# New tables of order for the two recurrences of an attention-with-memory training step

## The chip, the cores and the metric

The kernel runs on one core of a Trainium2 chip. The metric is the device time of one execution in microseconds. Three runs of the kernel before took 2881.65, 2874.34 and 2867.66 us, so the median is 2874.34 us. A separate execution was taken by the hardware profiler; all rows of the trace are from it.

The engines are named as the profile names them: PE multiplies matrices, PEld loads its weights, DVE, ACT and POOL work on vectors, and SP issues transfers between DRAM and the on-chip memory. Each engine runs its own instructions in the order in which the program lists them, and waits on semaphores for the others.

## The reference

The reference is one forward pass and its gradients. A layer norm of `x` (2048 tokens of 512) feeds two branches that are added to `x`: a dense layer with a squared relu, and an attention that runs over segments of 32 tokens and carries 8 memory rows from one segment to the next.

```python
for s in range(n_seg):                       # 64 segments of 32 tokens, 32 heads of 128
    h = concatenate([mem, xs])               # 8 memory rows and 32 tokens
    q, k, v = h @ Wq, h @ Wk, h @ Wv
    p = softmax(where(mask, q @ k.T * scale, -1e9))
    o = (p @ v) @ Wo
    mem, out = o[:8], o[8:]
...
return x + A(layernorm(x)) + B(layernorm(x))
```

The output and the gradients to ten inputs are returned. Since `mem` of one segment comes from the segment before, the forward pass is a chain of 64 steps, and its gradient is a chain of 64 steps in the other direction.

## The kernel before

The program has four parts: the dense branch, the forward recurrence, the backward recurrence, and a last part with the weight gradients and the layer norm's gradient. The change touches only the two recurrences.

**Steps and blocks.** Four segments make a block, so each recurrence has 16 blocks of four steps. The step of one segment is written by `chain` (L1510 for the forward pass, L1895 for the backward pass), and ends with small matmuls (L1574 and L1967) whose result a copy on DVE (L1578 and L1970) puts into the input of the next step. Beside the chain there is work of a block that no step waits for at once: `l_qkv` and `l_attn` for the 32 memory rows of the block, `dw_unit` with weight gradients of the dense branch, and in the backward pass `l_pre` and `l_post`. PE runs this work between the pieces of the chain.

**Where the plan's order comes from.** Every piece of work is given to `_Plan.add` (L427) with the engines on which it may run and the keys that it reads and writes. `_Beat.run` (L571) then sets the order. A table gives each piece of a block one number. The number divided by four is its place, in units of 10 ps, and the remainder chooses the engine where several are possible. A block is shifted by `_FWD_BEAT` or `_BWD_BEAT`. The pieces are taken from a heap by place, each as soon as all pieces that it depends on have been taken (L575 to L591), and written into the engines' streams in that order. So the numbers set an order and choose engines. They are no waits, and no time of them reaches the chip. Each recurrence has three tables: one for the blocks in the middle, one for the first block and one for the last.

**The pieces that the prediction follows.** In the backward pass `l_post` (L1801) works for a block that is already behind the chain. It calls `post` twice, with t=1 and t=2. Each call has four rows of loads (`load_x`, L1825): `xs` (256 KB from `S_Q` or `S_GON`) and `ys` (64 KB from `S_DSL` or `S_PL`). Two groups of 16 matmuls (L1852) each need two rows. Both calls use the same tiles, so the loads of t=2 can only start when the matmuls of t=1 are done. `load` (L1881) brings in `qN` (`XA<-S_Q`) and `kN` (`XA<-S_K`) for the next step, and `part_bd` (L1919) stores gradients (`S_GN<-XK`) for the last part. All these transfers are issued by SP, in one order.

In the forward pass `l_attn` stores `oLN` (`S_ONL<-XN`, L1500) from a tile into which the next block's `l_qkv` writes its first result; the copy that writes it must wait until the store has read the tile.

Of the kernel before, what the change touches and what calls it, by code (L numbers as in the profile page):

```python
# [29 lines left out]
        -35108400, -35109600, -34069200, -33215600, -34203599, -27704800, -27740400, -27741600, -27857600, -28116799,  # L30
        -22391600, -32365600, -34834799, -26164400, -34263999, -30979200, -31039600, -28224400, -28490000, -35299599,
        -24862400, -25241200, -24694800, -24696000, -23745199, -23655600, -27293600, -28702399, -24296000, -23041599,
        -24794400, -24795600, -24804400, -24862400, -23065199, -21676800, -20583200, -21155600, -19949600, -20989199,
        -18652400, -34074800, -37341200, -22558400, -21219600, -30884798, -22557600, -21218400, -22739998, -20980400,
        -28366398, -21035600, -21178799, -20605600, -19862000, -23279200, -19503199, -20900398, -20943198, -20102799,
        -20601998, -20944398, -25291598, -17164398, -22294798, -19283199, -24175997, -19087199, -24174797, -24467597,
        -19211598, -21183197, -21320797, -20775600, -24605198, -21543200, -21144400, -23337598, -21143200, -21144400,
        -21177599, -20788400, -22347998, -20771600, -20561999, -31007600, -19832400, -26897200, -17555199, -21206798,
        -20530798, -19731599, -21187198, -19222398, -18641598, -17183598, -19206798, -21250398, -22817199, -21321997,
        -17842399, -23020797, -23019597, -24468797, -23904799, -18536000, -16712398, -18133597, -28483597, -24721598,  # L40
        -16714798, -23417200, -18662000, -16232000, -17364000, -16018398, -17676799, -16228000, -18608398, -15828000,
        -18532798, -20371200, -17828800, -53166400, -22479600, -25422400, -11184000, -22650800, -14834800, -9430800,
        -27846000, -29697200, -14539200, -20660400, -27866000, -18134400, -19296800, -26897600, -17455600, -25411200,
        -32264400, -22280800, -18564000, -33130400, -16210800, -17698000, -25142800, -16899600, -14704800, -16240000,
        -12004800, -12012000, -20302000, -12007200, -12006000, -25868800, -11752400, -13070800, -20175200, -6536400,
        -8713200, -10025600, -6537600, -6171600, -12362800, -6540000, -5040000, -13676800, -6250800, -1146800,
        -15441200, -5170000, -1148000, -10122000, -3590000, 56800, -10009600, -3342400, 55600, -6087600, -2657200,
        573200, -4985199, -5052797, 1297201, 9000803, -1145600, -31999, -1979997, 2555600, 3227201, 2138803,
        -46612000, -41546397, -38099999, -29635598, -23431599, -22088399, -15200000, -15202400, -22613198, -15052400,
        -15051200, -29632799, -14813200, -14008398, -14838400, -17825599, -22861600, -13897200, -13094000, -22466799,  # L50
        -13347198, -13588798, -13111199, -12667198, -13144398, -12759598, -11490398, -12012398, -13987197, -15031197,
        -12011198, -13082799, -20575997, -17271999, -16903597, -16901999, -12015600, -11391998, -15051200, -15048800,
        -21121599, -15028400, -15029600, -17823199, -14466800, -17299999, -14423200, -13642798, -14468000, -12118000,
        -12119200, -21241599, -13139598, -13348398, -13092399, -12110398, -12112798, -12111598, -11683598, -11286398,
        -16066797, -15186397, -11947598, -15185197, -16157599, -22449599, -12741199, -15767197, -12007200, -11630398,
        -10745597, -22755997, -11401998, -16980398, -11753600, -12008400, -10721200, -11753600, -11232798, -10564799,
        -10301600, -9523198, -10300800, -9425598, -9757600, -16181600, -22719600, -14226400, -15694800, -18456000,
        -9370000, -10520000, 16840800, -13515198, -10210400, -10183600, -17245199, -10208800, -10302000, -17641998,
        -9415200, -9435999, -9414000, -16200398, -8681600, -8678800, -8154400, -10645999, -9479998, -9480798,
        -8328799, -10191598, -12689598, -10190398, -6047598, -6952798, -12719197, -9317598, -7609599, -10184397,  # L60
        -10191598, -6362799, -11621597, -8842397, -6360800, -6173198, -9859600, -10303200, -11002398, -9416000,
        -9417200, -9479999, -9268000, -17542799, -8806800, -11970398, -8676400, -7768000, -8155600, -6411999,
        -9482398, -10190398, -7783199, -9601598, -9600398, -9553198, -9507598, -9602798, -6302799, -19317597,
        -6374797, -9230797, -6221199, -9508798, -6829197, -5222799, -5076000, -6063198, -5104397, -23340397, -6070798,
        -5085598, -4551600, -4772000, -4626400, -4627600, -6497599, -6217998, -4131200, -6139198, -3946000, -3821598,
        -12406000, -8649600, -16295200, -15608800, -8648800, -5695200, -13044400, -4524800, 28582800, -3549600,
        -3553200, -5107598, -3551200, -3594800, -10185198, -3334800, -4316798, -3341200, -5105999, -2522000, -2397200,
        -1882400, -7007599, -5040398, -6653598, -6261999, -1571998, -1571998, -1570798, -1267998, 8802, -10331199,
        -8691197, -6289597, -1266798, -6259999, -5227199, -5084799, -6258797, -1506400, 446802, -3418000, -3419200,
        -5104799, -3536000, -3552400, -20737998, -2898400, -6402798, -3057600, -5086399, -1905600, -1355200, -1356400,  # L70
        -7977599, -5182398, -1764398, -3248399, -1441998, -1472398, -1492798, -37198, -361998, -6281997, -451598,
        -5972397, -7821597, -4999197, -5224399, -5990797, -3337199, -2988400, 452802, -6249597, -8347997, 435202,
        451602, 55600, 182800, 181600, -25200, 795602, 1229601, -3509600, 2090402, 1128800, 2176402, 2145600,
        -2782400, -18027600, -8857200, -1200, -5668800, 636000, 161600, 3070400, 471200, 7186802, 13911600, 23484800,
        -55200, 13365600, -17325600, -18465600, 3230800, 3899600, 122000, -6523600, 7050802, 8038402, 6965601,
        9318402, 3474802, -358398, 11142000, 8637602, 11321600, 11236800, 11319200, 11318000, 12418401, 12383601,
        5885600, 11175602, 10658402, 12636400, 2772400, 13057600, 13941600, 15736800, 16727600, 16725200, 16724000,
        17085201, 8694800, 13290800, 20578800, 22906403, 26035203, 9340800, 29804803, 24149203, 30399200, -40125200,
        -45562397, -13558400, -12482400, 10973602, 9985602, 5080000, -1928000, -8948000, -3944000, 7572003, 2804003,
        3576003, 1208003, -640000, -2712000, 2896000, 4788002, 460002, -531999, 9428002, -4391998, 7656002, 7748000,  # L80
        4748002, 19136000, 18468000, 18468000, 3896000, -3776000, 4360002, 13844002, 21888000, 21888000, 27368000,
        30636000, 28140000, 27296000, 22820000, 24276000, -291999, 37320003, 8000003, 8400003, -664000, 308001,
        -644000, -515998, -36000, -6283999, 64000, 464002, -1348000, -4723999, 64000, -9399998, 2328000, 3092002,
        2308000, 2656002, -7688000, 5680001, 2348000, -10039999, 132000, 8092001, 4892000, 6532002, 5368000, 3692001,
        -5344000, 9368002, 12660000, 18344002, 11404000, 8092001, 24936000, -5551999, -5595999, 5920000, -6795999,
        -991998, 5400000, -5587998, 4360002, 7476000, -5587998, -7139998, 8272000, 1712001, -5751998, 11356000,
        -16859998, -12599999, 12932000, -11211999, 6536002, 14852000, -11703999, -631998, 13096000, -6843998, 6504002,
        12468000, -395998, -1107999, 15328000, -6787998, -631998, 15904000, 5624001, -9979998, 15872000, -1723999,
        1332002, 14652000, -175999, 5220002, 18368000, -1903999, 2168001, 22100000, 940001, 2232002,
    ),  # L90
# [2109 lines left out]
```

## Time and profile before

| | us |
|---|---|
| median of 3 runs | 2874.34 |
| lowest and highest run | 2867.66, 2881.65 |
| the profiled execution, its own time | 2858.24 |
| span of the profiled execution, first to last instruction | 2856.5 |

The profiled execution was some 16 us shorter than the median run. Its span is 1.7 us shorter than its own time. A row of the trace's timeline has the start in us, the length in us, the engine, the line, the operation with what it writes and reads, and a count; in brackets stands how long the engine sat idle before it and what ended that. A row of the waits has who waited for whom, the total in us, how often, and the longest.

### The profile page before, as it was taken

To read this page: it belongs to the slowest core of one execution; us is meant where nothing else is said; L and a number is where in the kernel's file an instruction comes from. 1 tells how busy PE (TensorE), PEld (TensorE's weight loads), DVE (VectorE), ACT (ScalarE), POOL (GpSimd) and SP (SyncE) were. 2 spreads that over 40 slices of the span, in tenths; PEclk is the share of its full clock that TensorE was granted. 3 is DMA by queue.
4 is the path that set the end of the run, shared out by engine and by line. 5 is a ranking of instruction groups with operands and counts; after the bars stand their busy time and mean duration, and the time that the engine had idled before them with its cause. 6 is when DMAs were issued, how large, how long until landed. Compare 5 with 4: busy or idle time off the path is not lost.

```text
span 2856.5 us, 114006 instructions
## 1 busy us (share of the span) xinstructions
PE 2690.7 (94%) x47470; PEld 1553.5 (54%) x47640; DVE 1632.8 (57%) x4814; ACT 1168.5 (41%) x2761; POOL 929.7 (33%) x2595
## 2 busy tenths in 40 slices
PE   7998999999999999899899999999999999999999
PEld 5664565655656555655555555555555544444444
DVE  5644666666666666776666666666666602232322
ACT  4333454555555555554455455455555400000000
POOL 1112223223322223344444445444444301111111
PEclk9999999999999999999999999999999999999999
DMA  6657768777777764568888888998898899788861
GB/s 195 211 170 206 198 196 216 207 204 200 202 206 207 204 182 162 157 159 213 221 237 224 221 236 227 212 230 221 226 226 219 225 350 291 228 255 267 253 185 44
DMA packets 558171, 606.25 MB, mean 212 GB/s; under 512 B 229925, under 2 KB 359222, under 8 KB 555606
## 3 DMA queue, kind: packets, MB, share of 16 engines
q1 hardware_dynamic: 542486, 544.88, 69.5%
q0 software_dynamic: 15168, 54.08, 6.0%
q8 instruction: 373, 6.11, 0.9%
q14 instruction: 144, 1.18, 0.1%
HBM read 290.14 MB, written 272.12 MB: 197 GB/s over the span
## 4 chain that ended last, share of the span: by engine, by line
PE 28%; issue 10%; DVE 8%; DMA 5%; POOL 2%; ACT 2%; SPq 0%; DVEq 0%; POOLq 0%; ACTq 0%
PE ps L2137 12%; PE ps L1752 7%; PE ps L871 3%; PE ps L981 3%; DMA S_GN<-XK 1%; DMA WA<-S_GN 1%; DVE maskA L1938 1%; PE ps L757 1%; DVE XN L854 1%; DMA XN<-S_PL 1%; PE ps L1967 1%; DVE XA L1936 1%; DVE XN L761 1%; DVE PB L1943 1%; DVE PB L1942 1%
## 5 line engine op out<-in xcount | busy, mean ns | idle before, releaser
L871 PE MATMUL ps<-WA,PA 128*32 128x512 bf16 x6144 | 367.2, 380 | 4.7 <-DVE PA L1578 3.8
L2137 PE MATMUL ps<-WA,WB 128*128 128x512 bf16 x1505 | 330.7, 379 | 2.2 <-DVE gwo L761 0.6
L1752 PE MATMUL ps<-WA,XK 128*32 128x512 bf16 x5120 | 319.3, 383 | 5.5 <-DVE XK L854 3.4
L871 PEld LDWEIGHTS <-PA 128*32 128x32 bf16 x8192 | 206.9, 96 | 202.3 <-issue 15.7
L2137 PEld LDWEIGHTS <-WB 128*128 128x128 bf16 x1896 | 185.6, 98 | 224.6 <-issue 1.1
L997 POOL COPY BDA<-PB 32x128 bf16<-32x128 bf16 x484 | 139.9, 289 | 422.1 <-DVE PLp L1546 288.5
L761 DVE CAST gwo<-ps 128x512 bf16<-128x512 f32 x64 | 40.0, 684 | 401.7 <-PE ps L2137 268.3
L763 ACT CAST gwo<-ps 128x512 bf16<-128x512 f32 x64 | 33.2, 598 | 517.1 <-PE ps L2137 357.8
L763 ACT CAST XK<-ps 128x512 bf16<-128x512 f32 x313 | 180.4, 587 | 102.5 <-PE ps L981 42.1
L1752 PEld LDWEIGHTS <-XK 128*32 128x32 bf16 x5120 | 117.9, 97 | 145.6 <-DVE XK L854 44.8
L1752 PE MATMUL ps<-WA,XN 128*32 128x512 bf16 x2560 | 168.2, 382 | 0.5 <-issue 0.2
L2148 POOL DMA_DIRECT2D out_dram<-gwo x96 | 71.4, 751 | 295.4 <-ACT gwo L763 264.4
L761 DVE COPY XN<-ps 128x256 f32<-128x256 f32 (+1 forms) x148 | 66.5, 450 | 169.7 <-PE ps L757 118.5
L763 ACT CAST XA<-ps 128x512 bf16<-128x512 f32 (+1 forms) x154 | 90.3, 587 | 127.9 <-PE ps L871 114.9
L763 ACT COPY XN<-ps 128x512 bf16<-128x512 bf16 (+1 forms) x156 | 72.6, 477 | 158.1 <-PE ps L1752 54.4
L871 PE MATMUL ps<-WB,PA 128*32 128x512 bf16 x2048 | 127.5, 386 | 9.8 <-issue 9.0
L1417 PE MATMUL ps<-WB,OT 128*32 128x256 bf16 x4096 | 131.8, 274 | 4.8 <-DVE OT L854 3.8
L981 PEld LDWEIGHTS <-XK 128*128 128x128 bf16 x1536 | 95.1, 98 | 69.1 <-issue 21.2
L1630 PE MATMUL ps<-XA 128*128 128x512 bf16 x353 | 115.5, 381 | 10.3 <-issue 4.6
L1417 PEld LDWEIGHTS <-OT 128*32 128x32 bf16 x4096 | 101.4, 97 | 40.1 <-DVE OT L854 28.5
L854 DVE STREAM_TRANSPOSE XK<-XK 128x256 f32<-128x256 f32 x256 | 108.5, 434 | 24.8 <-ACT XK L763 21.9
L1003 POOL COPY BDA<-XA 32x256 bf16<-32x256 bf16 x256 | 107.2, 419 | 46.2 <-POOL XK L1003 13.9
(302 smaller groups left out, 5571.8 us busy)
## 6 DMA issues: line engine op xcount, KB each, us to landing
S_GN<-XK SPq DMA_DIRECT2D x192, 256.0 KB
WA<-S_GN SPq DMA_DIRECT2D x160, 256.0 KB
S_K<-kN SPq DMA_DIRECT2D x64, 256.0 KB
S_Q<-qN SPq DMA_DIRECT2D x64, 256.0 KB
S_V<-vN SPq DMA_DIRECT2D x64, 256.0 KB
S_ON<-oN SPq DMA_DIRECT2D x64, 256.0 KB
XA<-S_K SPq DMA_DIRECT2D x64, 256.0 KB
XA<-S_Q SPq DMA_DIRECT2D x64, 256.0 KB
```

Source lines behind the costliest of these rows:

```text
L761: nc.vector.tensor_copy(out, in_)
L763: nc.scalar.copy(out, in_)
L854: self.plan.add({"DVE": 0.36}, lambda e, x=x: nc.vector.transpose(dst[:, x, :, :].rearrange("p i c r -> p (i c r)").bitcast(F32).rearrange ...
L871: nc.tensor.matmul(bk()[32 * j:32 * (j + 1), :], lhsT=win(dc), rhs=Wt(dc, c0), start=(dc == 0), stop=(dc == DC - 1), tile_position=(0, 32 ...
L981: nc.tensor.matmul(bv()[:, n * P:(n + 1) * P], lhsT=B_[:, i, :, :].rearrange("p j k -> p (j k)"), rhs=X[:, i, :], start=(y == 0 and n == 0 ...
L997: self.plan.add({"ACT": 0.31, "DVE": 0.2, "POOL": 0.31}, lambda e, j=j: {"ACT": nc.scalar.copy, "DVE": nc.vector.tensor_copy, "POOL": nc.g ...
L1003: self.plan.add(cost or {"ACT": 0.4, "DVE": 0.27, "POOL": 0.42}, lambda e, j=j: {"ACT": nc.scalar.copy, "DVE": nc.vector.tensor_copy, "POO ...
L1417: nc.tensor.matmul(bk()[32 * t:32 * (t + 1), :], lhsT=tq(OTt, i, j), rhs=Wo[:, JQ * i + j, h * HB:(h + 1) * HB], start=(i == 0 and j < 2), ...
L1630: A(pe(0.217, "f", 0.11), lambda e, c=c, z=z, x=x: nc.tensor.matmul(bks[x]()[:], lhsT=anT[x][:, c, :], rhs=sx[z][:], start=(c == 0), stop= ...
L1752: nc.tensor.matmul(bk()[32 * j:32 * (j + 1), :], lhsT=tq(XT, i, j), rhs=wtf(t, i, j), start=(first and i == 0), stop=(last and i == NI - 1 ...
L2137: nc.tensor.matmul(bks[n]()[:], lhsT=HNc[:, rc, dc * P:(dc + 1) * P], rhs=half_of(gns[y], hf), start=(y == 0), stop=(y == NRC - 1))
L2148: q.dma_start(outWs[t][dc * P:(dc + 1) * P, hf, :, j], wt[:].rearrange("p (i e) -> p i e", i=4))
```

## The change

All six tables are replaced: three of `_FWD` (631, 493 and 515 numbers) and three of `_BWD` (724, 618 and 561). Both beats stay, and so does every line of code. The same pieces of work are therefore done with the same instructions; what changes is the order of the instructions on each engine and, for a part of the copies, the engine. The new numbers come from a search that also replays each schedule with two microseconds added to every transfer.

Nearly every number differs, so the diff is cut here to the heads and to the lines of the tables for the middle blocks that hold the loads followed above.

```diff
@@ -27,354 +27,356 @@
 
 _FWD = (
     (
...
-        5885600, 11175602, 10658402, 12636400, 2772400, 13057600, 13941600, 15736800, 16727600, 16725200, 16724000,
...
+        22049440, -21214998, 17848480, 17814360, 17976200, 17973800, 19018201, 19262921, 1923240, 13584802, -58674558,
...
 _FWD_BEAT = 5839300
 _BWD = (
     (
...
-        -7878360, 1441880, -332837, 12056923, 767040, 10570800, -20801400, -20374400, -32138240, -12133360, -46209360,
...
-        27711002, 31732600, 19858520, 38789560, 31832880, 32623360, 41521920, 31840040, 30816960, 8400240, 3455040,
...
+        9791040, -36825960, 23496720, -26575120, 3544040, -30169437, 10715403, 14217080, -2427160, -21531640,
...
+        36478400, 13092201, 30025682, 12236640, 42295722, 33332002, 36457080, -13086000, 22217080, 18799040, 35533000,
+        43214240, -18079040, 10092280, -7420480, -646120, 44170880, -3707199, 11543801, 24283520, 46068682, 47095842,
...
 _BWD_BEAT = 6498400
```

In `_FWD` the store `S_ONL<-XN` goes from 5885600 to 1923240. In `_BWD` the load of `qN` for the second step of a block goes from 767040 to 14217080, and that of `kN` from 10570800 to -2427160. The eight loads of `post` with t=2 (x and y of row 0, x and y of row 1, then its first matmuls, then x and y of rows 2 and 3) go from 19858520, 38789560, 31832880, 32623360 and 31840040, 30816960, 8400240, 3455040 to -13086000, 22217080, 18799040, 35533000 and -18079040, 10092280, -7420480, -646120.

665 rows, old and new, of tables (_BWD, _FWD) are left out of this document.

## The prediction

> **What bounds the kernel now.** I read the page first, then the rows of the two matmuls that end a step, then who waits for what inside the recurrences.
>
> ```profile
> span 2856.5 us, 114006 instructions
> PE 2690.7 (94%) x47470; PEld 1553.5 (54%) x47640; DVE 1632.8 (57%) x4814; ACT 1168.5 (41%) x2761; POOL 929.7 (33%) x2595
> PE 28%; issue 10%; DVE 8%; DMA 5%; POOL 2%; ACT 2%; SPq 0%; DVEq 0%; POOLq 0%; ACTq 0%
> ```
> ```profile
> L1574 PE MATMUL ps<-selF,RFA x1008: 179/183/204, 255.2 to 1173.8; 128*32 128x16 f32 x168
> L1967 PE MATMUL ps<-sel,XN x2016: 169/176/201, 1244.0 to 2266.7; 128*32 128x8 f32 x184
> ```
> ```profile
> 377.30:1089.00 711.70, 681.55 (x15613) 423.88 (x15695) 482.11 (x1436) 363.02 (x884) 207.28 (x576) 1.00 0.75 203
> 1305.70:2234.70 929.00, 862.12 (x19432) 496.59 (x19432) 600.97 (x1856) 478.66 (x1140) 445.53 (x1373) 0.99 0.87 224
> ```
>
> PE is busy 94% of the span, and the chain has DMA in it for 5%. The second fence places the recurrences: the last matmuls of a step start from 255.2 to 1173.8 in the forward pass and from 1244.0 to 2266.7 in the backward pass. With 62 steps between, a step takes 14.8 and 16.5 us. The third fence has, for a stretch inside each recurrence, its length, the busy time and count of PE, PEld, DVE, ACT and POOL, then clock, DMA share and GB/s. PE is idle for 711.70 - 681.55 = 30 us in the first, and for 929.00 - 862.12 = 67 us in the second. The clock is 1.00 and 0.99, so it isn't the reason. A new order of the same instructions can win only from such idle time, and the backward pass has most of it. Its waits for SP's transfers name one line:
>
> ```profile
>   PEld L1852: 24.8, 15
>   PE ps L1852: 23.0, 15
> ```
>
> These rows (who waited for the transfers of line 817 from 1245 to 2267; total, times) say that PE stood before the matmuls of `post` 15 times, for 23.0 us: once a block, 1.53 us each. PEld sees the same stops. One of them, in the timelines of SP and PE:
>
> ```profile
> 1370.95 0.38 SPq L817 DMA_DIRECT2D XN<-S_PL  x1
> 1371.38 0.42 SPq L817 DMA_DIRECT2D XN<-S_GON  x1
> ...
> 1372.85 0.38 SPq L817 DMA_DIRECT2D XA<-S_Q  x1
> 1373.32 1.73 SPq L817 DMA_DIRECT2D S_GN<-XK  x2
> 1375.15 0.46 SPq L817 DMA_DIRECT2D XA<-S_K  x1
> 1375.66 0.53 SPq L817 DMA_DIRECT2D XN<-S_PL  x1
> ...
> 1376.78 0.40 SPq L817 DMA_DIRECT2D XH<-S_PLL  x1
> ```
> ```profile
> 1367.78 0.61 PE L1852 MATMUL ps<-XN,XN 128*32 128x128 bf16 x16
> ...
> 1378.51 0.28 PE L1912 MATMUL ps<-XA,XN 128*32 128x40 bf16 x16
> 1380.86 0.70 PE L1852 MATMUL ps<-XN,XN 128*32 128x128 bf16 x26 [2.08 <-DMA XN<-S_PL]
> ...
> 1385.35 0.38 PE L981 MATMUL ps<-XA,BDB 128*128 128x128 bf16 x4
> ```
>
> The tiles come free when the matmuls of t=1 end, at 1367.78 + 0.61 = 1368.39. The y of row 0 is the last `XN<-S_PL`, issued only at 1375.66: SP has the next step's `qN`, two stores and `kN` ahead of it. PE is ready at 1378.51 + 0.28 = 1378.79 and goes on at 1380.86, which is 5.2 us after that issue. Such a stop isn't made up later. The next rows are the copies that begin and end two steps at the same place of their blocks, with the stop of the second:
>
> ```profile
> 1374.90 0.44 DVE L1970 CAST PA<-ps 128x16 bf16<-128x16 f32 x2 [0.65 <-PE ps L1967]
> 1393.57 0.17 DVE L1970 CAST PA<-ps 128x16 bf16<-128x16 f32 x1 [0.44 <-PE ps L1967]
> ...
> 1442.97 0.44 DVE L1970 CAST PA<-ps 128x16 bf16<-128x16 f32 x2 [0.65 <-PE ps L1967]
> 1459.49 0.17 DVE L1970 CAST PA<-ps 128x16 bf16<-128x16 f32 x1 [0.44 <-PE ps L1967]
> ```
> ```profile
> 1447.04 0.70 PE L1852 MATMUL ps<-XN,XN 128*32 128x128 bf16 x26 [0.18 <-DMA XN<-S_PL]
> ```
>
> The steps take 18.67 and 16.52 us, 2.15 apart; their stops are 2.08 and 0.18, 1.90 apart. What is taken from the stop is taken from the step.
>
> **The change part by part.** Nothing is added or removed, so each part is a wait that goes or comes. I sorted the pieces by the old and the new numbers, as the kernel does, and compared SP's order with PE's.
>
> *The loads of `post` with t=2.* The new numbers put all eight directly behind the matmuls of t=1, rows 0 and 1 first, before `kN` and the two stores; PE's own order between the two groups hardly changes. Issued from 1368.39 at 0.42 us each, as the row at 1371.38 has it, the four of rows 0 and 1 are out by 1370.1. With the 5.2 us of above they are in by 1375.3, 3.5 us before PE is ready. The last of the eight is out by 1371.8 and in by 1377.0. So I take the whole 23.0 us as gained. The gain is at least what a burst leaves of it (12.5, worked out with the first rival), and at most 23.0. Next late is then `qN`.
>
> *The load of `qN` for the second step of a block.* This one moves the wrong way: it now stands behind the two `S_GN` stores and behind `XH<-S_PLL`, whose issue at 1376.78 ends at 1377.2. Queued behind its landing on PE are the L981 matmuls of the chain itself, due at 1385.35 less the stop, 1385.35 - 2.08 = 1383.3. The longest landing that the chain of waits shows among its longest pieces of this kind is
>
> ```profile
> 1698.82 6.38 DMA XA<-S_V
> ```
>
> so `qN` comes between 1377.2 + 5.2 = 1382.4 (0.9 early) and 1383.6 (0.3 late). That costs 0 to 15 × 0.3 = 4.5 us; I take 2.
>
> *Forward: the store `S_ONL<-XN` and the loads of `dw_unit`.*
>
> ```profile
> ACT XN L763 <- DMA S_ONL<-XN: 32.5, 10, 5.4
> PE ps L757 <- ACT qN L763: 6.7, 5, 2.1
> PE ps L1630 <- DMA XA<-S_XN: 2.5, 3, 1.7
> ```
> ```profile
> 1041.61 0.43 SPq L817 DMA_DIRECT2D S_PL<-PLp  x1
> 1042.32 1.22 SPq L817 DMA_DIRECT2D S_ONL<-XN  x1
> ```
> ```profile
> 1046.62 0.58 ACT L763 CAST XN<-ps 128x512 bf16<-128x512 f32 x1 [5.35 <-DMA S_ONL<-XN]
> 1047.11 0.59 ACT L763 CAST qN<-ps 128x512 bf16<-128x512 f32 x1
> ```
>
> ACT waited for this store ten times, and behind the waiting copy stands the copy of `qN`, on which the chain's transposes on PE (L757) wait: 6.7 us in five places. In the new order the store `S_PL<-PLp` no longer stands ahead of `S_ONL`, and the copy of `kN`'s second half, which is needed later, stands behind the waiting one. The gain is between 0 (ACT's wait of 5.35 hardly shrinks with a store of 0.43 gone) and 6.7; I take 5, nearer the upper end, because `qN` itself is no longer behind that wait. The loads of `dw_unit` get more PE work between their release and their use, and I take 2 of the 2.5 us in the last of the waits (0 to 2.5).
>
> *Copies on other engines.* By the remainders, 29 more of the forward pass's pieces go to POOL (780 to 809), and the backward pass shifts 53 to ACT (1304 to 1357).
>
> ```profile
> L997 POOL COPY BDA<-PB 32x128 bf16<-32x128 bf16 x484 | 139.9, 289 | 422.1 <-DVE PLp L1546 288.5
> ```
>
> At 289 ns that is at most 29 × 0.289 = 8.4 us on POOL, most of it beside PE; POOL stands idle 422.1 us before this group alone. I take 2, between 0 and 8.4.
>
> *The end of the backward pass.* In the last block five large loads for the last part now stand on SP ahead of the last eight of `post`, at the old order four.
>
> ```profile
> 2291.05 0.58 PE L2050 MATMUL ps<-WB 128*128 128x512 bf16 x1 [1.39 <-DMA WB<-S_GN]
> ```
>
> One more load ahead can add a stop as long as this one or one of 5.2 us; or none, where the load is wanted next anyway. I take 2.
>
> The sum is -23.0 - 5 - 2 + 2 + 2 + 2 = -24 us. Against the profiled execution's own 2858.24 us that is 2834. Its 2858.24 lies 16.1 below the median of 2874.34 of the runs shown, and from that the same sum gives 2850 us.
>
> **The rivals.** *The burst.* All eight loads now go out together.
>
> ```profile
> S_GN<-XK SPq DMA_DIRECT2D x192, 256.0 KB
> ...
> XN<-S_GON SPq DMA_DIRECT2D x60, 256.0 KB
> ...
> XN<-S_PL SPq DMA_DIRECT2D x60, 64.0 KB
> ```
>
> Four of 256 KB and four of 64 KB are 1.28 MB. If they share the 224 GB/s of the backward row above, they need 5.7 us beside the 5.2 of one landing: 1368.4 + 10.9 = 1379.3. With the first group's rows as late as the last, PE, ready at 1378.79, stops for 0.5 us in each of 15 blocks; with 0.2 for the second group that is 15 × 0.7 = 10.5 us, so that 12.5 of the 23.0 is gained. For it speaks a DMA share of 0.87; against it that rows 0 and 1 go first. It gives 2850 + 10.5 = 2861.
>
> *Another reason for the stop.* If the y of row 0 were in long before 1380.86 and PE waited for something that the profile doesn't name, new places would win nothing there: 2850 + 23 = 2873. Against it speaks that the stop follows the last issue by 5.2 us. The Trainium skill's "DMA: Bandwidth & Descriptors", section "Latency and other measured facts", would have it so: it gives a fixed cost of about 2 us. By that rule a transfer of 64 KB issued at 1375.66 would be in before 1378.79 and the sum would be -1 us. The 5.2 us of the trace don't agree, and I give it 3 in 100.
>
> *`qN` in place of y: slower.* The wait of L981 would stand in the recurrence itself. If the landing of `qN` also waits for the two stores issued before it, 512 KB at 224 GB/s are 2.3 us more: in at 1382.4 + 2.3 = 1384.7, 1.4 late, 21 us in 15 blocks, which gives 2850 - 2 + 21 = 2869. Slower than before by 14.4 us needs (14.4 + 24 + 2) / 15 = 2.7 us each, a landing of 8.8 us after the issue, and gives 2889. For it speaks the place behind the stores; against it the 6.38 us. The Trainium skill's same page, section "Queues, rings and completion order", says that a transfer's semaphore counts only after the earlier writes of the same DMA engine have landed. By that rule the 1.4 us are the ones to expect; that y took 5.2 us behind two stores agrees with it, without showing it alone.
>
> *More than I count.* PE also stops for nothing that the profile shows, in steps where many transfers go out:
>
> ```profile
> PE ps L871 <- issue: 9.0, 6, 2.0
> ```
>
> If the calmer queue shortens these too, 9 us more go: 2841. Nothing in the order says that it must.
>
> **How the numbers follow.** A measurement of this kernel can tell about 0.5%, 14.4 us, from no change; that puts the bounds at 2860 and 2888.7. I give the forecast 0.50, more than counted 0.08, the burst 0.14, another reason 0.03, `qN` 1.4 late 0.14, and `qN` slower than before 0.11, with the new engines' copies among the doubts that it stands for. Faster is 0.50 + 0.08 = 0.58, the same 0.14 + 0.03 + 0.14 = 0.31, slower 0.11. The forecast's own range, from the bounds of its terms, is 2843 (all gains: -23.0 - 6.7 - 2.5, and no cost: -32) to 2860. The range of 2828 to 2877 adds the cases on both sides but the slower one, and the 14 us by which the runs before differ (2867.66 to 2881.65).
>
> **What would show it.** In the profile after, the 15 stops of PE before L1852 for `XN<-S_PL` would be gone, and the steps that had them would take some 16.5 us each. The eight loads of t=2 would follow each other on SP. PE's wait before L757 for ACT's `qN` would be under 2 us. The prediction is wrong if L981 waits for `XA<-S_Q` a block at a time, if L1852 still stops, or if the steps without a stop grow by a few tenths, which in 128 steps is the whole gain.

## The result and the profile after

Four runs of the changed kernel took 2845.15 to 2847.82 us, with a median of 2845.62 us. Four runs of the kernel before, beside them, had a median of 2873.06 us. The ratio is 0.9903 with an interval of 0.9878 to 0.9929: 27.4 us less. The profiled execution after took 2845.15 us itself, about as long as its runs.

Lines of the new kernel's code stand two higher than before (L1852 is L1854). The head of the page, and the matmuls that end a step:

```profile
span 2843.4 us, 114313 instructions
PE 2699.2 (95%) x47640; PEld 1550.4 (55%) x47640; DVE 1631.4 (57%) x4761; ACT 1190.9 (42%) x2804; POOL 939.6 (33%) x2605
PE 31%; DVE 10%; issue 8%; DMA 7%; ACT 2%; POOL 1%; SPq 1%; DVEq 0%; POOLq 0%; ACTq 0%
```
```profile
L1576 PE MATMUL ps<-selF,RFA x1008: 177/183/204, 254.6 to 1166.3; 128*32 128x16 f32 x168
L1969 PE MATMUL ps<-sel,XN x2016: 169/176/198, 1237.1 to 2252.9; 128*32 128x8 f32 x184
```

The recurrences now take 911.7 and 1015.8 us. In the first profile of before they took 918.6 and 1022.7, so each is only 6.9 us shorter, and the span 13.1 us shorter. That is half of what the medians say, so the kernel before was profiled a second time (the run `again`, below). This execution has a span near the median of its runs:

```profile
span 2867.7 us, 114006 instructions
```
```profile
L1574 PE MATMUL ps<-selF,RFA x1008: 179/183/204, 255.9 to 1179.8; 128*32 128x16 f32 x168
L1967 PE MATMUL ps<-sel,XN x2016: 169/176/198, 1251.1 to 2279.6; 128*32 128x8 f32 x184
```

Here the recurrences take 923.9 and 1028.5 us. Against this execution the new kernel has 12.2 us less in the forward pass, 12.7 less in the backward pass and 0.6 more in all the rest (915.3 to 915.9), 24.3 us in all. The backward pass in the second profile of before and in the profile after (length, then the busy time and count of PE and of the other engines, then the granted clock):

```profile
1251.10:2279.60 1028.50, 950.52 (x21369) 548.76 (x21373) 666.46 (x2048) 525.58 (x1255) 493.21 (x1521) 0.99 0.84 220
```
```profile
1237.10:2252.90 1015.80, 943.00 (x21367) 540.98 (x21363) 673.35 (x2019) 541.34 (x1307) 486.25 (x1499) 0.99 0.86 223
```

PE's idle time falls from 78.0 to 72.8 us only. The other 7.5 us of the 12.7 are time in which PE was busy with the same matmuls; part of that is the clock, to which the last section comes back.

Who waited for SP's transfers in the backward pass, in the second profile of before and in the profile after (total, times):

```profile
  ACT XK L763: 33.1, 23
...
  PE ps L1852: 28.8, 17
  DVE XK L761: 26.5, 13
```
```profile
  ACT XK L765: 31.1, 22
...
  PE ps L1854: 0.7, 1
```

PE's stops before the matmuls of `post` are gone in this stretch, 28.8 to 0.7 us. One stop of the last block lies behind it, where the profiles of before have 0.76 and 1.23 us:

```profile
2277.25 2.30 PE L1854 MATMUL ps<-XN,XN 128*32 128x128 bf16 x32 [3.95 <-DMA XN<-S_DSL]
```

A second thing is gone too, which the prediction did not look at: DVE no longer waits 26.5 us for a store out of XK. One block of the new kernel, in the timelines of SP and PE:

```profile
1486.93 1.25 SPq L1761 DMA_TRANSPOSE XA<-S_V  x1
1488.27 1.28 SPq L819 DMA_DIRECT2D XN<-S_GON  x2
1489.59 0.90 SPq L819 DMA_DIRECT2D XN<-S_PL  x2
1490.59 0.85 SPq L819 DMA_DIRECT2D XN<-S_GON  x2
1491.49 0.90 SPq L819 DMA_DIRECT2D XN<-S_PL  x2
...
1494.10 0.37 SPq L819 DMA_DIRECT2D S_GN<-XK  x1
...
1496.13 0.42 SPq L819 DMA_DIRECT2D S_GN<-XK  x1
...
1497.84 0.44 SPq L819 DMA_DIRECT2D XA<-S_Q  x1
```
```profile
1486.81 0.86 PE L1854 MATMUL ps<-XN,XN 128*32 128x128 bf16 x32
...
1499.31 0.50 PE L1854 MATMUL ps<-XN,XN 128*32 128x128 bf16 x12
...
1503.82 0.39 PE L983 MATMUL ps<-XA,BDB 128*128 128x128 bf16 x4
```

The eight loads go out in one row directly after the matmuls of t=1, as forecast, and PE's matmuls of t=2 at 1499.31 do not wait. The store at 1494.10 is that of `dN2`, the tile in which the next step's first gradient is put (`part_bd`, L1921): by the new numbers (5625040 to -37160200) it goes out as soon as it may, ahead of the store of `dN1` at 1496.13. In the old order it stood behind that store, behind `qN` and behind four loads of `post`.

Where time went back:

```profile
PE ps L983 <- DVE BDB L999: 11.6, 14, 1.2
...
PE ps L1914 <- ACT XN L765: 10.6, 9, 2.5
...
PE ps L1754 <- DVE XN L856: 6.0, 4, 2.4
```

The second of these was 1.2 us in the first profile of before (`PE ps L1912 <- ACT XN L763: 1.2, 2, 1.0` in the same view). Worked out from the starts of the copies that begin a step (L1970, now L1972), the step in which `post` of t=2 runs went from 18.9 us (second profile, mean of 14 middle blocks) to 16.6 us, and the step two behind it from 15.4 to 16.4 us (mean of all 15). The 14 middle blocks together went from 934.3 to 914.3 us. The first block, which has a table of its own, went the other way, from 61.2 to 66.2 us, and so did the first two steps of the last block, from 32.8 to 35.0.

In the forward pass, the two rows that answer to those of before:

```profile
ACT XN L765 <- DMA S_ONL<-XN: 44.3, 11, 6.2
...
PE ps L759 <- ACT XN L765: 3.1, 4, 1.3
```

ACT waits longer for the store than before (32.5 us), but `qN` no longer stands behind that wait: PE's stops before the transposes are 3.1 us, where `qN` and `kN` cost 6.7 + 1.8.

### The profile page after: what moved, and what is told of

Read it like the earlier page. It is cut to its first block, busy times and chain, and to the rows that moved or that the text cites. A ratio compares the mean times of both kernels' runs of the same rounds, so it can differ in the third digit from the quotient of the medians.

```text
span 2843.4 us, 114313 instructions
## 1 busy us (share of the span) xinstructions
PE 2699.2 (95%) x47640; PEld 1550.4 (55%) x47640; DVE 1631.4 (57%) x4761; ACT 1190.9 (42%) x2804; POOL 939.6 (33%) x2605
## 4 chain that ended last, share of the span: by engine, by line
PE 31%; DVE 10%; issue 8%; DMA 7%; ACT 2%; POOL 1%; SPq 1%; DVEq 0%; POOLq 0%; ACTq 0%
PE ps L2139 12%; PE ps L1754 8%; PE ps L873 4%; DMA S_GN<-XK 3%; PE ps L983 3%; PE ps L759 2%; DVE maskA L1940 1%; DMA XN<-S_GON 1%; ACT XK L765 1%; DVE XA L1938 1%; DVE XN L856 1%; DVE brA L1937 1%; DMA WA<-S_GN 1%; PE ps L1969 1%; DVE XA L1935 1%
## 5 line engine op out<-in xcount | busy, mean ns | idle before, releaser
L1754 PE MATMUL ps<-WA,XK 128*32 128x512 bf16 x5120 | 316.0, 381 | 12.4 <-DVE XK L856 8.5
L763 DVE CAST gwo<-ps 128x512 bf16<-128x512 f32 x64 | 40.1, 684 | 400.1 <-PE ps L2139 268.1
L765 ACT CAST XK<-ps 128x512 bf16<-128x512 f32 x330 | 189.2, 586 | 105.3 <-PE ps L983 58.3
L1754 PEld LDWEIGHTS <-XK 128*32 128x32 bf16 x5120 | 123.1, 96 | 149.2 <-DVE XK L856 40.5
L1754 PE MATMUL ps<-WA,XN 128*32 128x512 bf16 x2560 | 168.3, 387 | 6.9 <-DVE XN L856 6.0
L763 DVE COPY XN<-ps 128x512 bf16<-128x512 bf16 (+1 forms) x146 | 65.8, 450 | 155.8 <-PE ps L759 104.4
L999 ACT COPY BDA<-PB 32x128 bf16<-32x128 bf16 x452 | 133.4, 295 | 17.3 <-POOL BDA L1369 2.7
L765 ACT CAST XA<-ps 128x512 bf16<-128x512 f32 x141 | 82.9, 588 | 133.9 <-PE ps L873 114.3
L1632 PE MATMUL ps<-XA 128*128 128x512 bf16 x448 | 133.0, 381 | 0.9 <-DMA XA<-in_grad_out_dram 0.9
L765 ACT COPY XN<-ps 128x256 f32<-128x256 f32 (+2 forms) x158 | 73.8, 480 | 136.8 <-DVE XN L763 75.1
L983 PEld LDWEIGHTS <-XK 128*128 128x128 bf16 x1536 | 94.0, 97 | 58.1 <-POOL XK L999 26.7
```

The costliest lines, as they stand in the source:

```text
L763: nc.vector.tensor_copy(out, in_)
L765: nc.scalar.copy(out, in_)
L983: nc.tensor.matmul(bv()[:, n * P:(n + 1) * P], lhsT=B_[:, i, :, :].rearrange("p j k -> p (j k)"), rhs=X[:, i, :], start=(y == 0 and n == 0 ...
L999: self.plan.add({"ACT": 0.31, "DVE": 0.2, "POOL": 0.31}, lambda e, j=j: {"ACT": nc.scalar.copy, "DVE": nc.vector.tensor_copy, "POOL": nc.g ...
L1632: A(pe(0.217, "f", 0.11), lambda e, c=c, z=z, x=x: nc.tensor.matmul(bks[x]()[:], lhsT=anT[x][:, c, :], rhs=sx[z][:], start=(c == 0), stop= ...
L1754: nc.tensor.matmul(bk()[32 * j:32 * (j + 1), :], lhsT=tq(XT, i, j), rhs=wtf(t, i, j), start=(first and i == 0), stop=(last and i == NI - 1 ...
```

## The experiments

The halves swap all three tables of a pass; all other edits change numbers of the tables for the middle blocks and nothing else. Ratios are to runs of the kernel before beside them, and can differ a little from the ratio of two medians; the medians of before were 2868.3, 2870.1 and 2866.6 us in the three groups of runs.

### The kernel before once more (again)

No edit.

> The kernel before, unchanged, for a second profile. The profiled execution of before was 14.8 us shorter than the median of its runs (2858.24 against 2873.06), that of the kernel after was as long as its runs. If the executions of before differ by waits for transfers, this profile shows other sums in those waits: the 15 stops at L1852 for XN<-S_PL again near 23 us, and the rest of the difference in stops that the first profile had small. If they differ in something else (clock, the last part of the program), the two recurrences are as long as in the first profile, 918.4 and 1022.5 us.

It took 2869.46 us. The stops at L1852 are 28.8 us in this execution, against 23.0 in the first, and the forward pass is 5.3 us longer. There PE is idle only 1.9 us longer, and the granted clock lacks 5.1 us in place of 1.7 (over windows of 3.5 us, the length times what the clock lacks of 1.00, summed). So waits for transfers explain a part of the difference between the two executions, and the clock another. The first profile shows a lucky execution: its 2858.24 us lie near the low end of the runs of before, which went from 2856.5 to 2888.4 us over all groups. Part of why so few stops can move the whole time so far stands in the last section.

### One half of the tables at a time (only_bwd, only_fwd)

```diff
 only_bwd: _FWD of before, _BWD of after
 only_fwd: _FWD of after, _BWD of before
```

> The old tables of the forward pass with the new ones of the backward pass. If the loads of post are the main part, as forecast (23 of 29 us of gains), this has -15 to -20 us of the -27. If the backward pass gives only what the two profiles show (1022.5 to 1015.5 us), it is -7 us.

> The new tables of the forward pass with the old ones of the backward pass. As forecast (5 + 2 us): -7 us, as the two profiles have it too (918.4 to 911.4). If the forward pass carries the gain: -15 us or more, with the backward pass worth under 10.

`only_bwd` took 2854.2 us, ratio 0.9943 (0.9920 to 0.9965), `only_fwd` 2859.4 us, ratio 0.9967 (0.9949 to 0.9985): 14.1 and 8.9 us less than the 2868.3 beside them. Both halves gain, the backward one more, though 14.1 us is just under the 15 to 20 expected of it. The two add to 23 of the 27 us, or to 26 by the ratios.

### Only y row 0 in its new place (y0)

```diff
-        27711002, 31732600, 19858520, 38789560, 31832880, 32623360, 41521920, 31840040, 30816960, 8400240, 3455040,
+        27711002, 31732600, 19858520, 32623356, 31832880, 32623360, 41521920, 31840040, 30816960, 8400240, 3455040,
```

> The kernel before with one number changed: the load of y row 0 of post with t=2 (38789560 in the middle blocks) becomes 32623356, so that it is issued directly ahead of y row 1, before qN, the two S_GN stores and kN. If the stops at L1852 come from this place in the queue, they go from 23 us to under 3 (the first block's may stay), and the time falls by 14 to 21 us. If something else stood behind them, or another wait takes their place, the time stays within 5 us of before.

2872.3 us, ratio 1.0010 (0.9992 to 1.0029): nothing gained, as expected for the case that another wait takes the place of the first. This is the run that felled the forecast's main step. The stops did leave L1852, and came back at the next matmuls of the same step (waits, then the timelines of SP, DVE and PE in one block):

```profile
PE ps L1912 <- DVE XN L761: 24.8, 12, 3.7
PE ps L1852 <- DMA XN<-S_PL: 3.1, 1, 3.1
```
```profile
1382.61 0.85 SPq L817 DMA_DIRECT2D S_GN<-XK  x2
```
```profile
1388.66 0.69 DVE L761 CAST XK<-ps 128x512 bf16<-128x512 f32 x1 [2.77 <-DMA S_GN<-XK]
1389.27 0.42 DVE L761 COPY XN<-ps 128x512 bf16<-128x512 bf16 x1
```
```profile
1389.74 0.28 PE L1912 MATMUL ps<-XA,XN 128*32 128x40 bf16 x16 [2.21 <-DVE XN L761]
```

DVE wants to copy a new `dN2` into XK, and must wait until the store has read the old one. Behind that copy stands the copy to XN that PE needs at L1912. The store was issued at 1382.61 or just after and DVE went on at 1388.66. In the old kernel the same copy waited too, in the very stop that the prediction showed:

```profile
1379.46 0.69 DVE L761 CAST XK<-ps 128x512 bf16<-128x512 f32 x1 [1.62 <-DMA S_GN<-XK]
```

In `y0` PE goes on 1389.74 - 1388.66 = 1.08 us after this copy starts. The same 1.08 us after 1379.46 gives 1380.54, only 0.3 us before the 1380.86 at which y let PE go on. So two waits ended at nearly the same moment, and PE's rows name only the one that ended last.

### The copy of dN2 on ACT (act, y0_act)

The new tables also move this copy from DVE to ACT, so the next reading was that DVE's queue is the second cause.

```diff
 act:      entry 280 of _BWD, 3263162 -> 3263161
 y0_act:   the same, and y row 0 as in y0
```

> The kernel before with the copy of dN2 on ACT alone, y row 0 left at its old place. If two waits end together, this alone gains nothing: within 4 us of before, with the stops at L1852 for XN<-S_PL at 22 to 30 us as before. If the copy was the whole cause, it gains 15 us or more.

> The kernel before with two numbers changed: y row 0 directly ahead of y row 1, as in the run y0, and the first copy of dN2 in the next step (3263162 to 3263161, L1920) on ACT in place of DVE, as the new tables have it. In y0 the 25 us of stops came back before L1912, where DVE's copy to XN stands behind that copy to XK, which waits for the store S_GN<-XK. Theory: two waits ended together, and both must go. Then this run gains 15 to 25 us on before, L1852 stops for under 5 us and L1912 for under 8. Rival: the store holds ACT as it held DVE, a third wait follows in the same step, and the time stays within 5 us of before.

`act` took 2868.6 us, ratio 0.9997 (0.9981 to 1.0013): no difference, as expected, with 29.7 us of stops at L1852. `y0_act` took 2867.5 us, ratio 0.9982 (0.9962 to 1.0003). The expected 15 to 25 us did not come, and the rival that was written down did: the stops moved a second time, from L1912 to L1752, the matmuls that use the new `dN2` itself.

```profile
PE ps L1752 <- DVE XN L854: 25.2, 14, 3.5
```

DVE's wait for the store is gone (38.5 us in `y0`, 0.3 here), ACT's is not (46.9 and 48.1). So the wait is for the tile, whatever engine copies into it.

### The stores and loads moved in the old order (y0_gn, y0_dn2)

```diff
 y0_gn:    y0, and entries 620 to 623 and 225 (x and y of rows 2 and 3, qN)
           to places just behind the store of dN1
 y0_dn2:   y0, and entry 211 (store of dN2) 5625040 -> -37160200,
           entries 184, 225, 620 to 623 (store of dN1, qN, rows 2 and 3) behind it
```

> The kernel before with y row 0 ahead of y row 1, and the loads of rows 2 and 3 and of qN behind the first of the two S_GN stores; the copy of dN2 stays on DVE. If DVE's wait in y0 is for that store's place in the queue (issued at 1382.61, though its source was written by 1377.6), an issue some 2 us earlier takes most of the 25 us at L1912: 10 to 20 us faster than before. If the store lands late whatever its place, the time stays within 5 us.

> The kernel before with y row 0 ahead of y row 1, and the store of dN2 (S_GN<-XK, 5625040 to -37160200 as in the new tables) ahead of the store of dN1, of qN and of the loads of rows 2 and 3, which follow directly. All copies stay on their engines. Theory: the two things that end the stop of this step are the landing of y row 0 and the release of dN2's tile by its store, and the tables move both. In y0 the store could have gone out at 1379.7 and went out near 1383.0; 3.3 us earlier it is in before DVE wants the tile. Then the stops at L1852, L1912 and L1752 for y and for dN2 fall from 28 to under 8 us in all and the time by 15 to 25 us. Rival: another wait of the same step takes their place, and the time stays within 8 us of before, like that of y0_gn.

`y0_gn` took 2862.2 us, ratio 0.9985 (0.9964 to 1.0005). The stops shrank to 14.3 + 5.6 us:

```profile
PE ps L1912 <- DVE XN L761: 14.3, 13, 1.8
PE ps L1852 <- DMA XN<-S_PL: 5.6, 7, 2.2
```

The interval of the time reaches to no gain, and the 10 to 20 us did not come. The edit also did not do what its theory needs: in one block the store of `dN1` goes out at 1375.58, and that of `dN2` at 1380.12, still behind `qN` and the four loads. DVE's copy into the tile of `dN2` waits for the second: it starts at 1384.49, 4.4 us after that issue, against some 5.6 us in `y0`. `y0_dn2`, which puts the store of `dN2` ahead of these, was slower, which neither expectation had: 2879.7 us, ratio 1.0048 (1.0032 to 1.0063). Its waits and one block, SP and PE:

```profile
PE ps L1852 <- DMA XN<-S_PL: 30.5, 24, 2.0
```
```profile
1444.66 0.43 SPq L817 DMA_DIRECT2D XN<-S_PL  x1
```
```profile
1450.02 0.46 PE L1852 MATMUL ps<-XN,XN 128*32 128x128 bf16 x10 [2.00 <-DMA XN<-S_PL]
```

DVE's and ACT's copies hardly wait now, but rows 2 and 3 go out last and come 4.9 us after the end of their issue, too late for the second group of matmuls. In this stretch SP has no slack: in `y0` its transfers follow each other with about 0.1 us between them from 1373.1 to 1390.9. What stands last is late, and each of these edits mainly chose which transfer that was. To move all of them together in the old order was not tried.

### Undoing one number of the new tables (after_dve, after_late, after_y)

```diff
 after_dve:   entry 280 (copy of dN2 back on DVE)            -12120519 -> -12120518
 after_late:  entry 211 (store of dN2 behind that of dN1)    -37160200 -> 14037404
 after_y:     entry 616 (y row 0 behind the store of dN1)     22217080 -> 40031004
```

> The kernel after with one number changed: the first copy of dN2 in the next step back on DVE (-12120519 to -12120518). If the engine of this copy is a part of the gain, L1914 (L1912 before) waits for DVE's XN and the time rises by 5 to 20 us over after. If the new order has the stores early enough whatever the engine, it is within 4 us of after.

> The kernel after with one number changed: the store of dN2 directly behind that of dN1 (-37160200 to 14037404), y row 0 stays early. If the place of this store is one of the two causes, the 2.0 us by which it goes out later (1496.13 in place of 1494.10) come back as stops at L1914 or L1754, 20 to 35 us in 14 blocks: 2865 to 2880. If only y's place matters, it is within 4 us of after.

> The kernel after with one number changed: the load of y row 0 directly behind the store of dN1 (22217080 to 40031004), the store of dN2 stays early. If y's place is one of the two causes, it lands some 5.2 us after an issue near 1496.5, 2.4 us late, and L1854 stops 20 to 35 us in 14 blocks: 2865 to 2880. If the stores alone made the gain, it is within 4 us of after.

They took 2863.4, 2863.0 and 2859.9 us, with ratios of 0.9972 (0.9958 to 0.9987), 0.9997 (0.9980 to 1.0015) and 0.9979 (0.9962 to 0.9995). All three intervals lie apart from that of the new kernel (0.9878 to 0.9929). Against its 2845.6 us, measured beside other runs, that is 14 to 18 us lost by one number, and 20 to 27 us by the ratios. The 2847.1 us of the next run, measured beside the last two, say 13 to 16 us. The times of `after_late` and `after_y`, and the stops of `after_y`, lie below the ranges expected; the stops come back where they were expected. Each brings back its own stop, the other two stay away (one row of each kernel's waits, in the order above):

```profile
PE ps L1914 <- DVE XN L763: 16.6, 11, 3.0
```
```profile
PE ps L1754 <- DVE XN L856: 20.7, 12, 4.5
```
```profile
PE ps L1854 <- DMA XN<-S_PL: 17.7, 10, 5.1
```

So in the new tables each of three conditions is needed for the gain in this step: the rows of `post` are in, the store of `dN2` goes out first of the two, and DVE does not stand behind the tile.

### A try to win the rest (after_plus)

```diff
 entry 226 (kN behind the store of dN2)    -2427160 -> 13830000
 entry 657 (a transposing load)           -36435480 -> -35829276
```

> The kernel after with two numbers changed, to win what is left: kN of the second step behind the store of dN2 (-2427160 to 13830000), and the transposing load XK<-S_VM of every other block behind the store of the third step's dN2 (-36435480 to -35829276). In after, L1914 waits 10.6 us for ACT's XN, nearly all in the seven blocks that have that load ahead of the store, and L1754 waits 6.2 us for DVE's XN where dN2's store is late. If the store's place is what they wait for, 6 to 14 us go: 2832 to 2840. If the moved loads come late in their turn, the time is that of after or up to 10 us more.

2847.1 us, ratio 0.9928 (0.9906 to 0.9949): no better than the new kernel.

```profile
PE ps L1914 <- ACT XN L765: 12.4, 10, 3.3
PE ps L1754 <- DVE XN L856: 0.4, 1, 0.4
```

The first edit did what it should to its wait, 6.0 to 0.4 us, but the time did not fall with it. The second edit was a mistake: entry 657 is `XK<-S_VL` and its move changed nothing in the order of SP's transfers, so `XK<-S_VM` still stood ahead of the store, and the wait at L1914 stayed. What would become of it without that load ahead was not tried.

## Why the prediction came out right, and where it did not

The forecast was 2850 us, 24 us less than the median, with a range of 2828 to 2877; measured were 2845.6 and 27.4 us less. The time came out right, but not by the terms of the sum, and that its errors nearly cancel is luck. It takes 23 us of idle PE from the backward pass; there PE's idle time fell by 1.3 us against the first profile of before (74.1 to 72.8) and by 5.2 against the second.

*The loads of `post`.* That the 15 stops would go, and that the eight loads would follow each other on SP, was right (28.8 to 0.7 us). The step that failed is "what is taken from the stop is taken from the step", from which "I take the whole 23.0 us as gained" followed, with `qN` as the next thing late. `y0` shows that the stop is not taken from the step by moving y: the tile of `dN2` came free at about the same time and held PE just as long. What made the gain real was a second move that the prediction overlooked within its own diff, the store of `dN2` ahead of that of `dN1`, and a third, its copy on ACT. The prediction treated "the two stores" as one thing that the loads pass. The comparison of two steps that it used (2.15 us longer with 1.90 us more stop) shows that a stop lengthens a step; it does not show that nothing else would end at the same moment. The wait that does was in reach, in the view from which the row `PE ps L1852: 23.0, 15` was taken: DVE's copy to XK waited 20.9 us there for the same queue.

*`qN` for the second step.* The 2 us, and both rivals built on them, did not come. No L983 waits for `XA<-S_Q`: it is issued at 1497.84 and used at 1503.82, 6.0 us later, which is more than the 5.2 us that y row 0 took.

*The clock.* The prediction set it aside with "The clock is 1.00 and 0.99, so it isn't the reason", and let a gain come from idle time alone. That 0.99 is a term put at nothing: over the two recurrences the granted clock lacks 12.0 us in the first profile of before and 15.3 in the second, and 5.1 in the profile after. So of the 13.1 and 24.3 us between the profiles up to 7 and 10 go with the clock. A stop can cost twice, by its length and by a drop of the clock behind it (last section).

*The burst* and *another reason for the stop* did not come either: L1854 waits 0.7 us up to the last step, and `after_y` shows that y's place brings the stop back.

*Forward.* The rows agree with the mechanism: ACT's wait stays, what stands behind it changes. No edit tested it by itself. The gain was put at 5 + 2 us and is 8.9 us by `only_fwd`, 6.9 and 12.2 us by the two profiles, of which the clock can have 1.7 and 5.1. In all profiles this pass takes 918.6 to 925.1 us with the old tables (eight) and 910.1 to 914.4 with the new (six). The waits for the loads of `dw_unit` are 0.9 us, from 2.5 + 0.5.

*Copies on other engines.* The term of the sum that was mis-sized: 2 us were taken, and in its place stand new stops on PE for ACT's and DVE's copies (11.6 + 10.6 + 6.0 us in the rows above). The step two behind `post`'s grew by 1.0 us, some 15 us over the blocks. Not all of that is the copies: some 8 us are the stops at L1914, and some 6 us are work of PE that now runs in this step (busy 14.8 us before, 15.2 after) and no longer in the next (15.3 to 14.8). The stops at L983 lie mostly in that next step, those at L1754 in `post`'s. The prediction bounded this term by 29 more copies on POOL in the forward pass; the stops are in the backward pass, where ACT has 53 more pieces, and in part they are not the copies' own time but the store `S_GN<-XK` again, for which ACT's copies to XK wait 31.1 us.

*The end of the backward pass.* From the last L1967 (L1969) to the end it is 589.8 and 588.1 us before and 590.5 after, 0.7 or 2.4 us more, and the stop of 3.95 us in the last block did come. The 2 us were about right for this part. Not counted was that the first block and the first two steps of the last got longer, by 7 us against the second profile and 8 against the first.

So the larger gain of the step with `post` (2.3 us in each block, by the second profile) and of the forward pass, and the clock, paid for what the copies and the first and last block cost. Taking the sum from one profiled execution also hid that a usual run of before has larger waits than that one.

## What to carry to other kernels

When PE stops for one transfer, ask of every other engine what it waits for in that moment. If a second wait ends there too, moving the first gains nothing, and PE's own rows will name the second only once the first is gone. On a queue with no slack a moved transfer makes another one late, so an experiment that moves one number can show no gain although the number matters; undoing one number in the version that works is the test that tells. And a granted clock of 0.99 is not nothing: over 1000 us it is 10 us, and stops of 2 us can be what it comes from.

## What the runs showed of the hardware

A stop of PE can cost more than its length. In `y0` the same group of 32 matmuls follows a stop of 2.21 us in one block and of 1.06 us in another (windows with PE's busy time, the others', then the granted clock; below them the group in the timeline):

```profile
1389.70:1393.20 3.50, 3.39 (x52) 1.40 (x55) 3.08 (x12) 2.05 (x6) 2.32 (x6) 0.61 0.83 250
1524.70:1528.20 3.50, 3.38 (x76) 1.68 (x76) 3.08 (x12) 2.10 (x6) 2.37 (x6) 1.00 0.82 250
```
```profile
1390.09 3.32 PE L1752 MATMUL ps<-WA,XN 128*32 128x512 bf16 x32
```
```profile
1525.10 1.91 PE L1752 MATMUL ps<-WA,XN 128*32 128x512 bf16 x32
```

After the longer stop the granted clock is 0.61 over 3.5 us, and the group takes 1.4 us more. The clock's record behind these means has drops of one kind in the backward passes: 0.50 for 3.41 us, at most 1.7 us of PE's time each. All 82 drops of the 14 profiles begin on a grid of 3.413 us, one grid for each execution, and the window of the grid ahead of each holds 1.36 us or more of idle PE. All 38 windows with 2.2 us or more of idle PE are followed by a drop; between 1.36 and 2.2 us both happen.

The Trainium skill's "TensorE: Matmul & The Clock Gate", section "HAM oscillation — how this bites in real kernels", warns of idle gaps of more than about 3.4 us. Here 2.21 us was enough in one block, while after a stop of 2.34 us in the second profile of before the clock stayed at 1.00. The grid tells the two apart: the stop of 2.34 us, from 1318.06 to 1320.40, lies across the border of two windows, so that PE is idle for 1.29 us in one and 1.05 in the other (first two rows). A stop of the same profile that lies almost wholly in one window is followed by the drop (last two rows):

```profile
1315.94:1319.35 3.41, 2.12 (x57) 1.76 (x55) 0.72 (x2) 0.85 (x2) 0.92 (x4) 1.00 1.03 256
1319.35:1322.77 3.42, 2.37 (x67) 1.61 (x71) 2.59 (x8) 1.37 (x3) 1.04 (x1) 1.00 0.78 255
1780.15:1783.56 3.41, 0.17 (x16) 0.06 (x11) 0.52 (x1) 0.51 (x1) 0.79 (x4) 1.00 0.88 304
1783.56:1786.97 3.41, 3.16 (x68) 2.65 (x72) 2.36 (x8) 1.15 (x3) 1.03 (x1) 0.50 0.64 214
```

The two recurrences have seven such drops in the first profile of before, nine in the second and three in the one after. That fits the wide spread of the runs of before: of the 83 beside the experiments, the seven with a mean granted clock of 0.989 have a median of 2873 us, the six with 0.994 or 0.995 one of 2857. The new kernel's four runs have 0.994 to 0.996 and 2846, so that some 12 us remain at the same clock. No run here held everything else fixed, and a run with fewer stops has fewer drops too.
